# A list schedule planned with other durations, waits and priorities: clustered attention and an expert layer on one core

## The chip, the cores and the metric

The kernel runs on one core of a Trainium2 chip. A core has a tensor engine (PE in the profile), a vector engine (DVE), a scalar engine (ACT), GpSimd (POOL) and a queue that issues transfers (SP). Each engine works through its own queue in order; semaphores tie them together. The metric is the time of one execution on the device in microseconds, median of the runs shown.

## What is computed

Clustered attention over 4 batches, 8 heads, 768 tokens and 64 channels a head, followed by a layer with a rational activation. A query sees only the keys whose nearest centroid (of 16, by cosine) is its own.

```python
q_assign = np.argmax(np.einsum('bhsd,hcd->bhsc', q_n, c_n), axis=-1)
k_assign = np.argmax(np.einsum('bhsd,hcd->bhsc', k_n, c_n), axis=-1)
mask = q_assign[:, :, :, None] == k_assign[:, :, None, :]
scores = np.where(mask, scale * np.matmul(q, k.transpose(0, 1, 3, 2)), -1000000000.0)
attn = np.exp(scores - np.max(scores, axis=-1, keepdims=True))
attn = attn / (np.sum(attn, axis=-1, keepdims=True) + 1e-09)
x = np.matmul(attn, v)                    # then (3072 tokens, 512)
h = x @ w_in                              # (3072, 2048)
P = a[0] + a[1] * h + a[2] * h * h + a[3] * h * h * h
Q = 1.0 + np.abs(b[0]) * np.abs(h) + np.abs(b[1]) * h * h
out = (P / (Q + 1e-6)) @ w_out            # (3072, 512)
```

The weights arrive as float64 words.

## The kernel before

Every operand is split into two float16 parts (a high one and the rest), and each matrix product is made of three products of parts.

The work has four kinds. `weights` loads a chunk of w_in or w_out (8 chunks of 4 tiles), decodes the words on DVE, and splits them on ACT and POOL. `prep` prepares two heads of a batch: loads q, k and v, scales and splits them, finds the clusters, and turns the operands with DMA transposes. `v_scale` finds the scale of v in a batch from four loads of its own (tiles `rvm`); the loads for the work itself are `rv`, which has one buffer, so a pair's load waits until POOL has split the pair before it (`vlo`). `attend` handles two query tiles of each of two heads. `moe` handles 256 tokens in 8 groups of 256 hidden units.

For each of its 192 score tiles (4 batches x 4 head pairs x 6 query tiles x 2 heads) `attend` runs this chain. PE makes the scores (`s`, L861) into one of two score banks. DVE scales them and takes the row maximum (L877). ACT takes the exponential with the row sum (`su`). DVE makes the reciprocal in two small steps (L897, L902). The split follows: ACT writes the high part of the weights into `ah`, DVE writes the rest (L949). Then SP issues a DMA transpose of `ah` into `at` (L956), from which PE makes the product with v (`px`, L969). The tiles `ah` have two buffers, so ACT's part of a split waits until the transpose two tiles earlier has landed.

For each of its 96 groups `moe` makes `ph` on PE (L1028), two operations on ACT, a cubic on DVE (L1051, L1052), a square on POOL (L1057 to L1062), logarithm and exponential on ACT, a product on POOL (L1084), two more on DVE (L1099, L1106; every fifth of the former is on POOL), a split (`gh`, `gl`), and the product `po` on PE (L1127). All of a batch's four head pairs have to be done before its MoE begins, so the MoE of batch b runs beside the attention of batch b + 1, and the last one alone.

The order in each queue is set by a planner in the kernel (`Plan`). The body of the kernel only records operations: engine, an assumed duration in ns, tiles read and written, and a priority `vt`. `emit` then plays a list schedule over the engines with these durations: an operation is ready when its predecessors have ended and a time by engine (`LAT`) has passed; a transfer takes the issue time, a description time and its own duration; the rings of buffers and banks are counted. Of an engine's operations that can start within `look` ns the one with the least `vt` goes next:

```python
key = (max(start, now + self.look), o.vt, o.seq)
```

The order in which operations are picked is the order in which they are written to the program. The chip knows nothing of the assumed times: on it each engine runs its queue in that order and waits where it has to. `vt` counts MoE groups (8 a block of tokens, 24 a batch), shifted by an entry of the table `K` for the kind of operation, with further entries for the first batch (`.0`) and the last (`.3`).

Of the kernel before, what the change touches and what calls it, by code (L numbers as in the profile page):

```python
# [10 lines left out]
F32 = mybir.dt.float32  # L11
# [5 lines left out]
ALU = mybir.AluOpType  # L17
# [10 lines left out]
class Buf:  # L28
    """A tile that is allocated when the first operation on it is emitted."""
# [18 lines left out]
class Plan:  # L48
    """Records operations, then emits them in the order of a list schedule over the engines."""

    WINDOW = 3413.0
    LAT = {"PE": 200, "ACT": 155, "DVE": 130, "POOL": 80, "SP": 950}
# [5 lines left out]
    def op(self, eng, ns, fn, r=(), w=(), vt=0.0, claim=(), co=(), chain=None):  # L58
        """Reads r, writes w, reserves slots for claim. Of the tiles in co it writes a part of its own.
        Operations of a chain are emitted in their order."""  # L60
        o = Op()
        o.eng, o.ns, o.fn, o.vt, o.seq = eng, ns, fn, vt, len(self.ops)
        o.preds, o.succs, o.ready, o.after, o.then = set(), [], 0.0, None, []
        touched = {}
        for b in r:
            touched[b] = b.psum
        for b in w:
            touched[b] = True
        for b, wr in touched.items():
            if b not in co:  # L70
                o.preds.update(b.writers)
            if wr:
                o.preds.update(b.readers)
                if b in co and b.writers and not b.readers:
                    b.writers.append(o)
                else:
                    b.writers, b.readers = [o], []
            else:
                b.readers.append(o)
            b.left += 1  # L80
        for b in claim:
            if b not in touched:
                b.left += 1
                touched[b] = False
        o.preds.discard(o)
        if chain is not None:
            o.after = self.last.get(chain)
            self.last[chain] = o
        o.bufs = list(touched)
        self.ops.append(o)  # L90
        return o

    def emit(self):
# [15 lines left out]
        def slot_time(o):  # L109
            """When the ring slots that o still needs are free; None: not known yet."""  # L110
            t, need = 0.0, {}
            for b in o.bufs:
                if b.ring is None or b in held:
                    continue
                f = freed.setdefault(b.ring, [0.0] * b.cap)
                i = need.get(b.ring, 0)
                if len(f) <= i:
                    return None
                t = max(t, f[i])
                need[b.ring] = i + 1  # L120
            return t
# [3 lines left out]
        def clock(start, ns):  # L125
            """How long the tensor engine takes from start: half its clock after an idle window."""
            t = start
            while ns > 0:
                i = int(t // self.WINDOW)
                for n in range(max(warm) + 1, i + 1):  # L130
                    u = busy.get(n - 1, 0.0) / self.WINDOW
                    warm[n] = u > (0.46 if warm[n - 1] else 0.8)
                f = 1.0 if warm[i] else 2.0
                step = min(ns * f, (i + 1) * self.WINDOW - t + 1e-3)
                busy[i] = busy.get(i, 0.0) + step
                ns -= step / f
                t += step
            return t - start
# [50 lines left out]
def clustered_attention_moe_kernel(  # L189
# [53 lines left out]
    def half(b, i):  # L243
        """A part of b with its own dependencies; its operations claim b."""
# [978 lines left out]
```

## Time and profile before

| | us |
|---|---|
| median of 3 runs | 1087.58 (1087.26 to 1088.86) |
| span of the profiled execution | 1086.1 |
| DVE busy | 947.5 (87%) |
| PE busy | 846.7 (78%) |
| ACT busy | 790.9 (73%) |
| POOL busy | 729.9 (67%) |
| DMA queue, share of 16 engines | 67.9% |

The profiled execution took 1086.1 us from its first to its last instruction; what lies around it is the difference to the runs' own times, 1.5 us at the median. In the views below a tile's name stands without its buffer number, a line of the kernel as L949, and L303 is the helper through which all ACT operations are recorded, so that its groups are told apart by their tiles. A wait is written "engine, tile, line <- what released it". DMA share is the mean busy share of the core's 16 DMA engines.

### The profile page before, as it was taken

Reading aid. Unit: us, or ns where it says so; the run is one execution under the profiler, and the core shown is the slowest. Engines: PE = TensorE matmul, PEld = TensorE weight load, DVE = VectorE, ACT = ScalarE, POOL = GpSimd, SP = SyncE. Lnnn points to the kernel's source line nnn. Section 1 sums busy time; section 2 is a strip of 40 time slices with the busy share of each in tenths; the row PEclk is TensorE's granted clock in tenths of the full one; section 3 lists DMA queues with packets and bytes.
Section 4 is the critical chain, followed back from the end, with each engine's and each line's share of the span. In section 5 each row is a group of like instructions: output and inputs, shape, how many; then the busy total and the mean of one; then the engine's idle time right before and its main releaser. Section 6 shows DMA issues by size and latency. Waiting matters only on the chain. (4 is left out here: it accounts for less than half of the span.)

```text
span 1086.1 us, 19660 instructions
## 1 busy us (share of the span) xinstructions
PE 846.7 (78%) x6925; PEld 550.9 (51%) x6925; DVE 947.5 (87%) x1877; ACT 790.9 (73%) x1347; POOL 729.9 (67%) x741
## 2 busy tenths in 40 slices
PE   1244554556689898898988988988888889999997
PEld 1122332334455565555655565645655656576664
DVE  6488998878899898889999898989999999888886
ACT  3376765758878878678877878778888778776663
POOL 3656464637776878767897687848787888445553
PEclk9957676667899999999999999999999999999999
DMA  6499998899957777595786886686777675630000
GB/s 188 142 212 201 227 233 199 203 214 207 195 108 127 151 137 133 118 157 93 148 135 121 152 134 154 117 181 131 132 155 138 106 138 102 116 64 1 21 20 20
DMA packets 427922, 150.22 MB, mean 138 GB/s; under 512 B 404272, under 2 KB 420656, under 8 KB 427824
## 3 DMA queue, kind: packets, MB, share of 16 engines
q1 hardware_dynamic: 427824, 148.98, 67.9%
q8 instruction: 54, 0.88, 0.3%
q14 instruction: 44, 0.36, 0.1%
HBM read 41.98 MB, written 6.29 MB: 44 GB/s over the span
## 5 line engine op out<-in xcount | busy, mean ns | idle before, releaser
L861 PE MATMUL s<-sk,sq 128*128 128x384 f16 x768 | 176.4, 362 | 157.3 <-DVE ah L949 111.6
L1028 PE MATMUL ph<-x,win 128*128 128x256 f16 x2304 | 274.4, 276 | 7.1 <-DVE t L1052 3.0
L1028 PEld LDWEIGHTS <-win 128*128 128x128 f16 x2304 | 227.0, 99 | 53.1 <-issue 7.7
L1127 PE MATMUL po<-wout,gh 128*128 128x512 f16 x768 | 229.3, 380 | 1.0 <-ACT gh L1113 0.8
L303 ACT ACTIVATE s<-s,nm 128x768 f32<-128x768 f32 x192 | 167.5, 873 | 85.3 <-DVE s L877 72.2
L949 DVE SCALAR_TENSOR_TENSOR ah<-s,su,ah 128x768 f16<-128x768 f32 x192 | 190.8, 1010 | 40.1 <-ACT ah L303 39.2
L303 ACT ACTIVATE ah<-s,su 128x768 f16<-128x768 f32 x192 | 169.2, 899 | 47.2 <-DMA at<-ah 22.1
L877 DVE TENSOR_SCALAR_CACHE_REDUCE s<-s,cc 128x768 f32<-128x768 f32 x192 | 192.4, 1017 | 11.8 <-PE s L861 11.4
L861 PEld LDWEIGHTS <-sq 128*128 128x128 f16 x768 | 69.9, 104 | 239.7 <-DVE ah L949 137.0
L1127 PE MATMUL po<-wout,gl 128*128 128x512 f16 x384 | 146.2, 381 | 5.4 <-POOL gl L1116 3.5
L969 PE MATMUL px<-at,vhi 128*64 128x256 f16 x1152 | 115.7, 297 | 15.7 <-DMA at<-ah 9.8
L1057 POOL TENSOR_SCALAR s<-u,gk 128x512 f32<-128x512 f32 x84 | 80.5, 958 | 66.0 <-ACT u L303 65.7
L1060 POOL TENSOR_TENSOR s<-s,u 128x512 f32<-128x512 f32 x84 | 113.7, 1353 | 7.0
L1084 POOL TENSOR_TENSOR s<-s,u 128x512 f32<-128x512 f32 x72 | 96.8, 1348 | 30.2 <-ACT u L303 29.8
L1116 POOL TENSOR_TENSOR gl<-t,gh 128x512 f16<-128x512 f32 x72 | 86.2, 1201 | 43.9 <-ACT gh L1113 28.0
L1127 PEld LDWEIGHTS <-gh 128*128 128x128 f16 x768 | 73.5, 98 | 71.8 <-issue 2.9
L969 PEld LDWEIGHTS <-vhi 128*64 128x64 f16 x1152 | 73.2, 118 | 41.3 <-issue 14.0
L969 PE MATMUL px<-at,vlo 128*64 128x256 f16 x576 | 93.1, 294 | 0.0
L1106 DVE SCALAR_TENSOR_TENSOR t<-s,t 128x512 f32<-128x512 f32 x84 | 85.6, 1020 | 3.6 <-POOL s L1084 1.5
L1099 DVE SCALAR_TENSOR_TENSOR t<-t,gk,u 128x512 f32<-128x512 f32 x70 | 68.4, 980 | 2.1 <-ACT u L303 2.1
L1052 DVE SCALAR_TENSOR_TENSOR t<-t,gk,ph 128x512 f32<-128x512 f32 x84 | 62.8, 748 | 3.0
L303 ACT ACTIVATE t<-ph,gk 128x512 f32<-128x512 f32 x84 | 65.0, 778 | 0.0
(177 smaller groups left out, 1477.8 us busy)
## 6 DMA issues: line engine op xcount, KB each, us to landing
rwi<-in_moe_w_in_dram SPq DMA_DIRECT2D x16, 512.0 KB, 4.6
rwo<-in_moe_w_out_dram SPq DMA_DIRECT2D x16, 512.0 KB, 5.0
rv<-in_v_dram SPq DMA_DIRECT2D x16, 384.0 KB, 4.1
rq<-in_q_dram SPq DMA_DIRECT2D x32, 192.0 KB, 3.0
rk<-in_k_dram SPq DMA_DIRECT2D x32, 192.0 KB, 3.2
rvm<-in_v_dram SPq DMA_DIRECT2D x16, 384.0 KB, 4.1
out_dram<-ob SPq DMA_DIRECT2D x24, 256.0 KB, 2.3
at<-ah SPq DMA_TRANSPOSE x192, 4.1
```

The costliest lines, as they stand in the source:

```text
L303: lambda: nc.scalar.activation(out=out(), in_=in_(), func=func, **{a: (x() if callable(x) else x) for a, x in kw.items()}),
L861: nc.tensor.matmul(sc.ap[:, i, :SH], lhsT=st["q" + x].ap[:, j, t, :], rhs=st["k" + x].ap[:, j, ks, :].rearrange("p t c -> p (t c)"), start ...
L877: lambda nm=nm, view=view: ts(out=view(), in0=view(), scalar1=cc.ap, scalar2=None, op0=ALU.mult, op1=ALU.min, accum_out=nm.ap),
L949: lambda part=part, view=view, su=su: stt(out=part(1), in0=view(), scalar=su.ap, in1=part(0), op0=ALU.mult, op1=ALU.subtract),
L969: nc.tensor.matmul(px.ap[j * D : (j + 1) * D, :], lhsT=vv.ap[:, j, kt, :], rhs=at[j].ap[:, p_, kt].rearrange("p t c -> p (t c)"), start=(i ...
L1028: nc.tensor.matmul(ph.ap[:, fi * TW : (fi + 1) * TW], lhsT=win[:, wpart, c, f * P : (f + 1) * P], rhs=xs[c].ap[:, xpart], start=(i == 0), ...
L1057: nc.gpsimd.tensor_scalar(out=s.ap, in0=u.ap, scalar1=col("b1r")(), scalar2=col("b0r")(), op0=ALU.mult, op1=ALU.add)
L1060: nc.gpsimd.tensor_tensor(out=s.ap, in0=s.ap, in1=u.ap, op=ALU.mult)
L1084: lambda u=u, s=s: nc.gpsimd.tensor_tensor(out=s.ap, in0=s.ap, in1=u.ap, op=ALU.mult),
L1106: lambda t=t, s=s: stt(out=t.ap, in0=s.ap, scalar=2.0, in1=t.ap, op0=ALU.subtract, op1=ALU.mult),
L1116: lambda gl=gl, t=t, gh=gh, e=(nc.vector if tail else nc.gpsimd): e.tensor_tensor(out=gl.ap, in0=t.ap, in1=gh.ap, op=ALU.subtract),
L1127: nc.tensor.matmul(po[ti].ap, lhsT=gg.ap[:, cs], rhs=wout[:, wpart, f, :], start=(i == 0 and f % (cw if apart else NF) == 0), stop=(i == 2 ...
```

## The change

No operation is added, removed or changed, and every engine's queue has as many rows after as before (PE 13747, DVE 1677, ACT 1108, POOL 734, SP 384). What changes is what the planner assumes:

- `LAT`, the time from an operation's end to its successor on another engine, is raised for ACT, DVE and POOL.
- The assumed durations of nearly all operations are replaced. Those of ACT and DVE are set to what the profile shows for the group, less 93 ns on ACT and 65 ns for each some 700 ns on DVE, taken off in `op`. The transposes go from 1344 to 2200 ns, half of an attention product (`px`) from 1296 to 1000.
- The table `K` has new numbers for nearly every kind of operation, `look` among them. Counts of buffers (`xn`, `NR`, `stk`) and shares of work between engines (`ghd`, `mulp`, `vsc`, `sgp`, `scp`) keep their values.
- Comments and docstrings are dropped; two line breaks move the numbers by two (L949 is L951 in the new file).

```diff
-    LAT = {"PE": 200, "ACT": 155, "DVE": 130, "POOL": 80, "SP": 950}
+    LAT = {"PE": 200, "ACT": 200, "DVE": 170, "POOL": 100, "SP": 950}
...
         o = Op()
+
+        ns -= {"ACT": 93, "DVE": 65 * max(1, round(ns / 700))}.get(eng, 0)
         o.eng, o.ns, o.fn, o.vt, o.seq = eng, ns, fn, vt, len(self.ops)
...
-    K = {'ghd': 0.25, 'p3': -265.35, 'max': -78.8, 'exp': -49.35, 'po': 3.6,
...
+    K = {'ghd': 0.25, 'p3': -1644.51, 'max': -150.93, 'exp': 33.42, 'po': 1831.34,
...
                 dve(
-                    925,
+                    1156,
                     lambda nm=nm, view=view: ts(
...
                 act(
-                    880, view, view, AF.Exp, [nm], [sc, su], u + kb("exp", b),
+                    1071, view, view, AF.Exp, [nm], [sc, su], u + kb("exp", b),
...
-                        784, lambda part=part: part(0), view, AF.Identity, [sc, su], [ah], u + kb("split", b), chain="split",
+                        899, lambda part=part: part(0), view, AF.Identity, [sc, su], [ah], u + kb("split", b), chain="split",
...
-                        930,
+                        1010,
                         lambda part=part, view=view, su=su: stt(
...
                 op(
-                    "SP", 1344,
+                    "SP", 2200,
                     lambda ah=ah, j=j, ti=ti: nc.sync.dma_start_transpose(
...
-            op("PE", 9 * 144, lambda k0=k0: av(k0, k0 + 3), [vhi, vlo, *at], [px], u, [x])
+            op("PE", 1000, lambda k0=k0: av(k0, k0 + 3), [vhi, vlo, *at], [px], u, [x])
...
             dve(
-                602,
+                932 if tail else 1020,
                 lambda t=t, s=s: stt(out=t.ap, in0=s.ap, scalar=2.0, in1=t.ap, op0=ALU.subtract, op1=ALU.mult),
```

Two places show what moves. The first is DVE's queue in the attention of batch 2 (tiles of a batch's number stand with it: `ah2_1_1_1` is batch 2, pair 1, query tile 1, head 1), beside the MoE of batch 1 (`t1_1_3` is its second block, group 3). Before:

```order
L877 TENSOR_SCALAR s2_1_1_1_6929,nm2_1_1_1_6942<-s2_1_1_1_6929,cc2_1_5512 128x2x384
L877 TENSOR_SCALAR s2_1_2_0_6936,nm2_1_2_0_6957<-s2_1_2_0_6936,cc2_1_5512 128x2x384
L702 TENSOR_SCALAR qsc2_3_6974<-sumq2_3_6955 128x1
L1051 SCALAR_TENSOR_TENSOR t1_1_3_6944<-ph1_1_3_6886,gk1_2539,t1_1_3_6944 128x512
L1052 SCALAR_TENSOR_TENSOR t1_1_3_6944<-t1_1_3_6944,gk1_2539,ph1_1_3_6886 128x512
L897 TENSOR_SCALAR su2_1_1_1_6959<-su2_1_1_1_6959 128x1
L1106 SCALAR_TENSOR_TENSOR t1_1_2_6780<-s1_1_2_6726,t1_1_2_6780 128x512
L897 TENSOR_SCALAR su2_1_2_0_6986<-su2_1_2_0_6986 128x1
L902 RECIPROCAL su2_1_1_1_6959<-su2_1_1_1_6959 128x1
L902 RECIPROCAL su2_1_2_0_6986<-su2_1_2_0_6986 128x1
L949 SCALAR_TENSOR_TENSOR ah2_1_1_1_7008<-s2_1_1_1_6929,su2_1_1_1_6959,ah2_1_1_1_7008 128x768
L949 SCALAR_TENSOR_TENSOR ah2_1_2_0_7019<-s2_1_2_0_6936,su2_1_2_0_6986,ah2_1_2_0_7019 128x768
```

After, around the same tile:

```order
L1054 SCALAR_TENSOR_TENSOR t1_1_1_6821<-t1_1_1_6821,gk1_2548,ph1_1_1_6716 128x512
L899 TENSOR_SCALAR su2_1_1_0_6849<-su2_1_1_0_6849 128x1
L879 TENSOR_SCALAR s2_1_1_1_6826,nm2_1_1_1_6868<-s2_1_1_1_6826,cc2_1_5508 128x2x384
L904 RECIPROCAL su2_1_1_0_6849<-su2_1_1_0_6849 128x1
L1101 SCALAR_TENSOR_TENSOR t1_1_0_6638<-t1_1_0_6638,gk1_2548,u1_1_0_6606 128x512
L1108 SCALAR_TENSOR_TENSOR t1_1_0_6638<-s1_1_0_6613,t1_1_0_6638 128x512
L899 TENSOR_SCALAR su2_1_1_1_6872<-su2_1_1_1_6872 128x1
L951 SCALAR_TENSOR_TENSOR ah2_1_1_0_6886<-s2_1_1_0_6781,su2_1_1_0_6849,ah2_1_1_0_6886 128x768
L904 RECIPROCAL su2_1_1_1_6872<-su2_1_1_1_6872 128x1
L879 TENSOR_SCALAR s2_1_2_0_6905,nm2_1_2_0_6916<-s2_1_2_0_6905,cc2_1_5508 128x2x384
L951 SCALAR_TENSOR_TENSOR ah2_1_1_1_6913<-s2_1_1_1_6826,su2_1_1_1_6872,ah2_1_1_1_6913 128x768
L704 TENSOR_SCALAR qsc2_3_6949<-sumq2_3_6919 128x1
```

Before, the split of `ah2_1_1_1` stands behind the two reciprocals of its pair, with nothing but the other tile's reciprocal between its own and itself; two maxima, then two reciprocals, then two splits stand together. After, the tiles of a pair are staggered, and a row maximum stands between this tile's reciprocal and its split.

The second place is SP's queue in the start, around the first transpose of attention weights (`at0_0_0_0`; `rwo` are w_out's words, `rwi` those of w_in, `sq2` and `sk2` the turned operands with the clusters). Before:

```order
L755 DMA_TRANSPOSE sq20_0_338<-tq20_0_151 128x12x128
L755 DMA_TRANSPOSE sk20_0_341<-tk20_0_161 128x12x128
L317 DMA rvm0_0_343<-in_v_dram 128x2x384
L317 DMA rvm0_1_365<-in_v_dram 128x2x384
L317 DMA rvm0_2_390<-in_v_dram 128x2x384
L317 DMA rvm0_3_428<-in_v_dram 128x2x384
L956 DMA_TRANSPOSE at0_0_0_0_444<-ah0_0_0_0_421 128x12x128
L755 DMA_TRANSPOSE sk10_1_450<-tk10_1_430 128x12x128
L317 DMA rk0_2_457<-in_k_dram 128x384 x2
L755 DMA_TRANSPOSE sq10_1_466<-tq10_1_446 128x12x128
L317 DMA rq0_2_468<-in_q_dram 128x384
L317 DMA rwi2_0_479<-in_moe_w_in_dram 128x1024
```

After:

```order
L319 DMA rwo3_0_259<-in_moe_w_out_dram 128x1024
L319 DMA rwo3_1_263<-in_moe_w_out_dram 128x1024
L319 DMA rwo3_2_353<-in_moe_w_out_dram 128x1024
L757 DMA_TRANSPOSE sq20_0_359<-tq20_0_151 128x12x128
L757 DMA_TRANSPOSE sk20_0_362<-tk20_0_161 128x12x128
L319 DMA rwo3_3_366<-in_moe_w_out_dram 128x1024
L319 DMA rv0_1_374<-in_v_dram 128x2x384
L319 DMA rwo2_0_382<-in_moe_w_out_dram 128x1024
L319 DMA rv0_2_443<-in_v_dram 128x2x384
L958 DMA_TRANSPOSE at0_0_0_0_454<-ah0_0_0_0_437 128x12x128
L319 DMA rwo2_1_459<-in_moe_w_out_dram 128x1024
L757 DMA_TRANSPOSE sk10_1_480<-tk10_1_435 128x12x128
```

Before, the four loads for v's scale (`rvm0`) stand ahead of the first transpose of attention weights. After, they have moved ahead of all of w_out's words, and the loads of v for the second and third pair (`rv0_1`, `rv0_2`) stand ahead of that transpose.

## Rows read from the trace of the kernel before

**Rows 1.** the page, part 1: busy us, share of the span, instructions

```profile
PE 846.7 (78%) x6925; PEld 550.9 (51%) x6925; DVE 947.5 (87%) x1877; ACT 790.9 (73%) x1347; POOL 729.9 (67%) x741
```

**Rows 2.** busy us by stretch: PE, PEld, DVE, ACT, POOL, PEclk, DMA share, GB/s

```profile
0.00:50.00 50.00, 7.95 (x83) 5.43 (x84) 27.96 (x67) 15.55 (x27) 25.31 (x31) 1.00 0.57 164
50.00:300.00 250.00, 135.48 (x1116) 83.15 (x1114) 210.68 (x480) 175.83 (x323) 143.80 (x170) 0.69 0.94 209
300.00:950.00 650.00, 575.90 (x4831) 377.22 (x4830) 598.20 (x1174) 517.04 (x872) 495.13 (x494) 0.99 0.72 133
950.00:1087.00 137.00, 127.41 (x904) 85.09 (x900) 110.62 (x160) 82.49 (x127) 65.65 (x46) 1.00 0.10 25
```

**Rows 3.** chain that ended last, after 950 us: start us, us, what

```profile
966.99 2.59 PE po L1127 x12
969.58 2.62 PE ph L1028 x24
```

**Rows 4.** waits of DVE, whole span: us in total, times, longest us

```profile
DVE ah L949 <- ACT ah L303: 39.2, 50, 2.6
...
DVE s L877 <- PE s L861: 11.4, 19, 1.7
DVE su L897 <- ACT s L303: 9.5, 20, 1.3
```

**Rows 5.** waits of DVE from 300 to 950 us, the fourth and the last

```profile
DVE t L1099 <- ACT u L303: 2.1, 3, 1.1
...
DVE km L694 <- PE kt L692: 0.2, 1, 0.2
```

**Rows 6.** instructions of DVE at 600 us: start us, us, what [idle before]

```profile
599.61 0.68 DVE L1106 SCALAR_TENSOR_TENSOR t<-s,t 128x512 f32<-128x512 f32 x1
...
600.44 0.28 DVE L902 RECIPROCAL su<-su 128x1 f32<-128x1 f32 x2
603.28 1.02 DVE L949 SCALAR_TENSOR_TENSOR ah<-s,su,ah 128x768 f16<-128x768 f32 x1 [2.55 <-ACT ah L303]
```

**Rows 7.** instructions of ACT at 602 us, the same columns

```profile
602.35 0.90 ACT L303 ACTIVATE ah<-s,su 128x768 f16<-128x768 f32 x1 [1.50 <-DMA at<-ah]
```

**Rows 8.** waits of ACT, whole span

```profile
ACT ah L303 <- DMA at<-ah: 22.1, 30, 2.2
```

**Rows 9.** the page, part 6: DMA issues, us to landing

```profile
at<-ah SPq DMA_TRANSPOSE x192, 4.1
```

**Rows 10.** groups by line: busy us, mean ns | idle before

```profile
L949 DVE SCALAR_TENSOR_TENSOR ah<-s,su,ah 128x768 f16<-128x768 f32 x192 | 190.8, 1010 | 40.1 <-ACT ah L303 39.2
...
L303 ACT ACTIVATE ah<-s,su 128x768 f16<-128x768 f32 x192 | 169.2, 899 | 47.2 <-DMA at<-ah 22.1 <-DVE su L902 8.3 <-issue 6.2
...
L1106 DVE SCALAR_TENSOR_TENSOR t<-s,t 128x512 f32<-128x512 f32 x84 | 85.6, 1020 | 3.6 <-POOL s L1084 1.5 <-POOL t L1093 0.8
...
L1099 DVE SCALAR_TENSOR_TENSOR t<-t,gk,u 128x512 f32<-128x512 f32 x70 | 68.4, 980 | 2.1 <-ACT u L303 2.1
```

**Rows 11.** issues of SP in the start

```profile
46.69 8.53 SPq L317 DMA_DIRECT2D rvm<-in_v_dram  x4
56.70 1.27 SPq L956 DMA_TRANSPOSE at<-ah  x1
```

**Rows 12.** instructions of DVE at 417 us

```profile
417.32 1.67 DVE L1106 SCALAR_TENSOR_TENSOR t<-s,t 128x512 f32<-128x512 f32 x1
...
418.98 2.06 DVE L1106 SCALAR_TENSOR_TENSOR t<-s,t 128x512 f32<-128x512 f32 x1
```

**Rows 13.** instructions of POOL at 417 us

```profile
416.73 1.71 POOL L1084 TENSOR_TENSOR s<-s,u 128x512 f32<-128x512 f32 x1
418.41 2.08 POOL L837 TENSOR_TENSOR vlo<-rv,vhi 128x768 f16<-128x768 f32 x1
```

More of the change, by code (lines that the diff above doesn't have):

```diff
@@ L693, in prep @@
         m1 = buf([1, 1], F32, "m1", f"km{n}", 4)
-        dve(200, lambda: nc.vector.tensor_reduce(out=m1.ap, in_=pt.ap[0:1, :], axis=AX.X, op=ALU.max), [pt], [m1], u)
+        dve(270, lambda: nc.vector.tensor_reduce(out=m1.ap, in_=pt.ap[0:1, :], axis=AX.X, op=ALU.max), [pt], [m1], u)
         pb = misc([P, 1], F32, f"kb{n}")
-        op("PE", 65, lambda: nc.tensor.matmul(pb.ap, lhsT=ones[0:1, :], rhs=m1.ap, start=True, stop=True), [m1], [pb], u)
+        op("PE", 235, lambda: nc.tensor.matmul(pb.ap, lhsT=ones[0:1, :], rhs=m1.ap, start=True, stop=True), [m1], [pb], u)
         qs, ks = buf([P, 2], F32, "qsc", f"qsc{n}", 2), buf([P, 2], F32, "ksc", f"ksc{n}", 2)
@@ L749, in prep @@
                 )
-            dve(270, lambda nm=nm, hi=hi: nc.vector.tensor_copy(out=cols(nm + "2", 0), in_=cols(nm + "1", hi)), [one], [two], u)
+            dve(500, lambda nm=nm, hi=hi: nc.vector.tensor_copy(out=cols(nm + "2", 0), in_=cols(nm + "1", hi)), [one], [two], u)
         def turn(x, u):
             op(
-                "SP", 1344,
+                "SP", 2200,
                 lambda x=x: nc.sync.dma_start_transpose(
@@ L784, in prep @@
         u = vt + kb("p3", b, 3)
-        dve(465, lambda: nc.vector.tensor_reduce(out=mx.ap, in_=ptl.ap, axis=AX.X, op=ALU.max), [ptl], [mx], u)
-        dve(469, lambda: tt(out=df.ap, in0=ptl.ap, in1=spread(mx), op=ALU.is_ge), [ptl, mx], [df], u)
+        dve(548, lambda: nc.vector.tensor_reduce(out=mx.ap, in_=ptl.ap, axis=AX.X, op=ALU.max), [ptl], [mx], u)
+        dve(553, lambda: tt(out=df.ap, in0=ptl.ap, in1=spread(mx), op=ALU.is_ge), [ptl, mx], [df], u)
         op(
-            "POOL", 960,
+            "POOL", 1109,
             lambda: nc.gpsimd.tensor_tensor(
@@ L793, in prep @@
         )
-        dve(469, lambda: nc.vector.tensor_reduce(out=mx2.ap, in_=df.ap, axis=AX.X, op=ALU.max), [df], [mx2], u)
-        dve(469, lambda: tt(out=oh.ap, in0=df.ap, in1=spread(mx2), op=ALU.is_equal), [df, mx2], [oh], u)
+        dve(541, lambda: nc.vector.tensor_reduce(out=mx2.ap, in_=df.ap, axis=AX.X, op=ALU.max), [df], [mx2], u)
+        dve(917, lambda: tt(out=oh.ap, in0=df.ap, in1=spread(mx2), op=ALU.is_equal), [df, mx2], [oh], u)
         NCP = D // NCL
@@ L832, in prep @@
         else:
[L833 to L834 removed]
+            act(933, rvf, rvf, AF.Identity, [ev], [rv], vt + kb("p4", b, 4), scale=lambda: ev.ap[:, 1:2])
+            act(832, lambda: flat(vhi), rvf, AF.Copy, [rv], [vhi], vt + kb("p4", b, 4), chain="vhi")
         op(
[L836 removed]
+            "POOL", 1717,
             lambda: nc.gpsimd.tensor_tensor(out=flat(vlo), in0=rvf(), in1=flat(vhi), op=ALU.subtract),
@@ L901, in attend @@
                     )
-                dve(75, lambda su=su: nc.vector.reciprocal(out=su.ap, in_=su.ap), [], [su], u + kb("su", b))
+                dve(157, lambda su=su: nc.vector.reciprocal(out=su.ap, in_=su.ap), [], [su], u + kb("su", b))
                 ah = buf([P, 2, S], F16, "ah", f"ah{nn}", kn("ah", 2))
```

111 lines of the change are left out of this document (54 added, 57 removed).

## The prediction

> **What bounds the kernel now.** I read the busy shares first. VectorE (DVE) is busy 947.5 us, 87% of the span, ahead of TensorE with 78% [rows 1]. So I look for the time in which VectorE stands still: 1086.1 - 947.5 = 138.6 us. The table by stretches [rows 2] divides it. In the first 50 us 22.0 us are idle, while the first loads land. From 50 to 300 us (weights decoded beside the attention of batch 0) 39.3 us are idle, and the DMA share is 0.94: there the transfers are almost as full as VectorE (210.7 of 250). From 300 to 950 us (MoE of batches 0 to 2 beside the attention of batches 1 to 3) 51.8 us of 650 are idle, with a DMA share of 0.72 and TensorE at 575.9. After 950 us only the 24 groups of the last MoE are left, and there TensorE is the bound: 127.4 of the 136.1 us that remain, in a strict alternation of 2.62 us (ph) and 2.59 us (po) a group [rows 3]; 24 times 5.21 is 125.0 us.
>
> The change moves no work from one engine to another (every queue has as many rows after as before), so it can win only VectorE's idle time, and the waits say which. The longest by far is the split of the attention weights, L949, waiting for ScalarE's half of the same split: 39.2 us in 50 waits; the reciprocal's first step waits 9.5 us for the exponential, and the row maximum 11.4 us for the scores [rows 4]. In the 300 to 950 stretch ten further kinds of wait, from L1099's 2.1 us to km's 0.2, make 13.3 us together [rows 5].
>
> One such wait shows the mechanism. VectorE ends the two reciprocals (L902) at 600.72 us, and the next thing in its queue is the split of the same tile, which starts at 603.28 after 2.55 us of standing [rows 6]. ScalarE's half needs 0.90 us and began only at 602.35, 1.50 us late, because its output buffer was still being read by a DMA transpose [rows 7]. That second cause occurs 30 times, 22.1 us [rows 8]: there are two `ah` buffers, and a transpose takes a median of 4.1 us to land [rows 9]. So VectorE stands where the order puts the split too soon after its own reciprocal, or too soon after the split two tiles earlier.
>
> **The change part by part.** Names and dependencies stay; the numbers in the plan change and with them each queue's order. I count a queue's order with durations of this trace: the k-th row of VectorE's old order is its k-th instruction in the trace, so every wait has its place in the order.
>
> *Term 1, the split's wait.* For each tile I add the durations of VectorE's rows that stand between the reciprocal and the split (each by the mean of its group, as [rows 10], less the 0.07 us or so by which a row overlaps the next). Of 190 tiles of the old order (the first two left out), 23 have less than 0.7 us there, and these waited 22.0 us in sum, 0.96 each. 36 have 0.7 to 1.2 us and waited 7.2 us, 0.20 each. The other 131 waited 9.4 us, 0.07 each. So the count sorts the waits well: it should, since ScalarE's half lasts 0.899 us [rows 10] and both handoffs come on top. In the new order the same three classes hold 7, 27 and 156 tiles: 7 x 0.96 + 27 x 0.20 + 156 x 0.07 = 23 us, against 38.6: 15.3 us less. The buffers say the same: under 5.5 us from the split two tiles earlier are 30 tiles in the old order (18.1 us of the waits) and 11 in the new one. About a third, 5.4 us, lies in the start before the first MoE group, where the transfers are full; I take half of that, since a split that comes earlier there meets a transpose queued behind loads. Term 1 is 9.9 + 2.7 = 12.6 us. Its bounds: 0, if the next wait in line takes all of it, and 29, if the waits fall in the ratio in which the time missing below 1.2 us falls (29.5 us to 11.1 in sum) and the rest is hidden too.
>
> *Term 2, the neighbours in the same chain.* From row maximum to reciprocal the time missing below 1.2 us falls from 9.0 to 7.4 us in sum; by that ratio the 9.5 us become 7.8: 1.7 us. From a split to the maximum two tiles later (two score banks) the time missing below 1.5 us falls from 21.4 to 18.8; the 11.4 us become 10.0: 1.4 us. Bounds 0 and 21.
>
> *Term 3, the ten small kinds.* I have no count for them. They lie between 0 and 13.3 us [rows 5]; I take a quarter, 3.3 us, as the two ratios of term 2 (a fifth and an eighth) are the nearest thing to them and term 1's is larger.
>
> *The start.* SP's new order loads the four tiles for v's scale before the w_out tiles, and puts the loads of v for the second and third pair in front of the first transpose of attention weights. v has one buffer, so the third pair's load stands until GpSimd has split the second pair's v, and the transpose waits behind it. In the old trace SP spent 46.69 to 55.2 us on the four scale loads, ahead of that transpose at 56.70 [rows 11]; these now come sooner. The two effects have opposite signs and a like size, some 8 us by this row. I book 0, bounds -8 and +8.
>
> *The end.* The first groups of the last MoE stand at the same place behind the same last attention tiles, and TensorE's rows are the same. The new order runs ph of two groups, then po of two, where the old one alternates one and one. With the same work and a bound engine I book 0. What covers it are VectorE's 110.6 busy us against TensorE's 127.4 [rows 2]; if pairs cost half a microsecond each for want of a finished `gl`, that is 12 x 0.5 = 6 us more.
>
> Sum: 12.6 + 3.1 + 3.3 = 19.0 us. The profiled span of 1086.1 becomes 1067.1; the median of the runs, 1087.58, lies 1.5 us above that span, so **1068.6 us**.
>
> [...] The table of durations is made of means, and one of them is no property of its operation. L1106 takes 0.68 us in one call [rows 6], 1.67 and 2.06 us in two calls that start while GpSimd's L1084 and L837 are running [rows 12, 13], and 1.02 in the mean [rows 10]. [...]
>
> **The rivals.**
>
> *A, overlap with GpSimd takes the gain (slower).* L1106 and L1099 are 84 + 70 = 154 calls. If the new order sets them beside GpSimd more often, busy time grows where I count on idle time: 19.0 us over 154 calls, 0.12 us a call, decides. At 0.2 us a call the time is 1068.6 + 30.8 = 1099 us. For it: the plan gives each call one duration whatever runs beside it, and the spread from 0.68 to 2.06 us is there. Against it: the calls and GpSimd's load are the same, and GpSimd is busy 495 of 650 us in the middle [rows 2], so a call meets it about as often in any order. Chance 0.11.
>
> *B, the waits return (no change).* What VectorE no longer waits for at L949 it waits for at the next row, because something behind it, the DMA transposes or the scores, sets the pace. Time 1087 us. For it: ScalarE's late start above was itself a DMA's. Against it: between 300 and 950 us neither DMA (0.72) nor TensorE is full. Chance 0.08.
>
> *C, the whole chain is freed (faster than forecast).* The split's waits fall by 29 us, those of term 2 by 4, the small ones by 5, and the start counts in full: 38 us, 1050 us. For it: VectorE is 92% busy in the middle, so 52 us are there to be had. Against it: 37 us must come from waits of which the count moves less than half. Chance 0.16.
>
> **How the numbers follow.** The forecast (19.0 us won, give or take the 8 us of the start and the 6 of the end, so 5 to 27) has 0.65. Faster by over 0.2% (about what a measurement of this kernel can tell from no change, 2.2 us) are the forecast and C: 0.81. Within it is B: 0.08. Slower is A: 0.11. The predicted time is the forecast's, 1068.6. The range leaves out A and what might lie beyond C: it goes from 1049 us, just under C, to B's 1087.
>
> **What would show it.** Right: in the new profile L949 waits about 23 us for ScalarE instead of 39, the waits of ScalarE's half for the transposes fall from 22 to some 12 us, VectorE's idle time between 300 and 950 us falls from 52 to about 37, and its busy sum stays within 10 us of 947. A would show as L1106 and L1099 with means above 1.14 and 1.10 us and a busy sum over 965. B would show as the same idle sum under other names, with L877 waiting for scores. An end that TensorE needs more than 131 us for, or a first MoE group later than now, would make the terms that I booked at 0 wrong.

## The result and the profile after

The changed kernel takes 1076.86 us (median of 4 runs, 1075.24 to 1077.87) where the kernel before took 1087.42 us beside it (median of 4 runs): a ratio of 0.9901, with a 95% interval from 0.9884 to 0.9918. That is 10.6 us won; 19.0 were forecast, and the time lies in the range. The profiled execution took 1075.5 us, against 1086.1.

In the changed kernel every line number is 2 higher: L949 is L951, L877 is L879, L897 is L899, L1051 is L1053, L1099 is L1101, L1106 is L1108. The page's part 1 answers to [rows 1]:

```profile
PE 851.7 (79%) x6925; PEld 555.1 (52%) x6925; DVE 938.3 (87%) x1877; ACT 790.6 (74%) x1347; POOL 711.3 (66%) x741
```

and the four stretches to [rows 2]:

```profile
0.00:50.00 50.00, 9.60 (x83) 5.80 (x84) 27.72 (x70) 21.13 (x39) 23.96 (x31) 1.00 0.71 198
50.00:300.00 250.00, 144.12 (x1169) 91.18 (x1170) 216.66 (x493) 176.92 (x321) 152.88 (x178) 0.71 0.97 206
300.00:950.00 650.00, 582.04 (x4905) 383.49 (x4905) 599.55 (x1178) 521.97 (x883) 488.75 (x493) 0.98 0.72 134
950.00:1087.00 137.00, 115.98 (x774) 74.63 (x770) 94.39 (x138) 70.55 (x106) 45.71 (x41) 0.98 0.03 12
```

VectorE's idle time is 1075.5 - 938.3 = 137.2 us, and it was 138.6. The gain on the page is 9.2 us of busy time and 1.4 of idle time, though the change was to win idle time. Between 300 and 950 us VectorE is idle 50.5 us; it was 51.8, and some 37 were forecast. The waits of VectorE over the whole span show why (us in total, times, longest), beside [rows 4]:

```profile
DVE ah L951 <- ACT ah L305: 23.4, 35, 2.0
DVE s L879 <- PE s L863: 16.1, 21, 2.5
DVE t L1053 <- ACT t L305: 11.5, 14, 1.3
DVE sk L1053 <- ACT sk L305: 8.6, 9, 1.9
...
DVE su L899 <- ACT s L305: 6.7, 15, 1.1
```

The wait at the split went from 39.2 to 23.4 us, which is what term 1 counted. But VectorE waits 4.7 us more for scores, and the first polynomial step now waits 20.1 us for ScalarE (t and sk), where it waited 2.2 us before. ScalarE's wait for the transposes, which answers to [rows 8], fell little:

```profile
ACT ah L305 <- DMA at<-ah: 19.3, 17, 3.8
```

Of the groups by line, these two answer to L1106 and L1099 in [rows 10] (busy us, mean ns, idle before):

```profile
L1108 DVE SCALAR_TENSOR_TENSOR t<-s,t 128x512 f32<-128x512 f32 x84 | 75.1, 896 | 4.5 <-POOL t L1095 2.6
...
L1101 DVE SCALAR_TENSOR_TENSOR t<-t,gk,u 128x512 f32<-128x512 f32 x70 | 73.9, 1057 | 3.6 <-ACT u L305 3.4
```

Fixed windows hold different work in the two kernels, so I cut both spans at points of the work: the first polynomial step of the first MoE group and of the last batch. The windows of VectorE (length, busy us, instructions, then TensorE's granted clock, DMA share and GB/s) before:

```profile
0.00:271.60 271.60, 215.08 (x502) 0.74 0.87 203
271.60:945.80 674.20, 617.63 (x1210) 0.98 0.72 135
945.80:1086.10 140.30, 114.75 (x167) 1.00 0.13 30
```

and after:

```profile
0.00:263.90 263.90, 211.38 (x491) 0.73 0.91 204
263.90:932.80 668.90, 617.95 (x1225) 0.97 0.74 139
932.80:1075.50 142.70, 108.99 (x165) 0.99 0.11 26
```

The start is 7.7 us shorter, the middle 5.3 us shorter with the same busy time, and the end 2.4 us longer, although VectorE is busy 5.8 us less there. In idle time of VectorE that is 4.0 us less, 5.6 less and 8.2 more, so the sum over the span hides what the first two stretches won. A stretch of one profile is sure to some 3 us only: in the profile of a later run with the same order up to the last split, the start took 267.0 us and the middle 671.7. In the middle, between those two points, VectorE's longest waits were before:

```profile
DVE ah L949 <- ACT ah L303: 25.8, 30, 2.6
DVE s L877 <- PE s L861: 4.4, 6, 1.7
DVE su L897 <- ACT s L303: 4.3, 11, 1.0
```

and are after:

```profile
DVE ah L951 <- ACT ah L305: 13.4, 23, 2.0
DVE s L879 <- PE s L863: 8.9, 13, 2.5
DVE t L1053 <- ACT t L305: 3.9, 7, 1.3
DVE t L1101 <- ACT u L305: 3.4, 5, 1.3
DVE t L1108 <- POOL t L1095: 2.6, 2, 1.8
DVE tk L746 <- ACT tk L305: 2.6, 2, 2.4
DVE su L899 <- ACT s L305: 2.5, 7, 0.6
```

The split's wait fell by 12.4 us there and all waits together only from 48.5 to 43.3 us: other waits in the same queue grew by 7.2 us. The two orders differ everywhere, so these rows alone do not show that it is the same time that moved; the third buffer below, which leaves the order as it is, comes nearer to that.

In the end the chain that ended last shows the pairs (start us, us, what):

```profile
965.91 5.24 PE ph L1030 x48
971.15 5.18 PE po L1129 x24
...
991.99 2.60 PE po L1129 x12
...
996.01 0.58 ACT ob L305
...
996.63 2.10 PE po L1129 x6
```

A pair costs TensorE what two groups cost in [rows 3], 5.24 for 2 x 2.62 and 5.18 for 2 x 2.59. What is lost lies between: from 994.59 to 996.63 us TensorE does nothing, until ScalarE has copied a finished product out of its bank (`ob`).

### The profile page after: what moved, and what is told of

Read it like the earlier page. It is cut to its first block, busy times and chain, and to the rows that moved or that the text cites. A ratio compares the mean times of both kernels' runs of the same rounds, so it can differ in the third digit from the quotient of the medians.

```text
span 1075.5 us, 19599 instructions
## 1 busy us (share of the span) xinstructions
PE 851.7 (79%) x6925; PEld 555.1 (52%) x6925; DVE 938.3 (87%) x1877; ACT 790.6 (74%) x1347; POOL 711.3 (66%) x741
## 4 chain that ended last, share of the span: by engine, by line
DVE 30%; PE 30%; ACT 12%; issue 10%; DMA 8%; POOL 8%; SPq 1%; ACTq 0%; DVEq 0%; POOLq 0%
PE ph L1030 11%; PE po L1129 11%; DVE ah L951 7%; DVE s L879 6%; PE s L863 4%; DMA at<-ah 4%; ACT ah L305 3%; PE px L971 3%; DVE t L1053 2%; DVE t L1101 2%; ACT u L305 2%; ACT s L305 2%; DVE t L1054 2%; DVE t L1108 2%; DVE tq L746 1%
## 5 line engine op out<-in xcount | busy, mean ns | idle before, releaser
L863 PE MATMUL s<-sk,sq 128*128 128x384 f16 x768 | 180.2, 364 | 134.6 <-DVE ah L951 109.1
L951 DVE SCALAR_TENSOR_TENSOR ah<-s,su,ah 128x768 f16<-128x768 f32 x192 | 192.8, 1010 | 24.6 <-ACT ah L305 23.4
L879 DVE TENSOR_SCALAR_CACHE_REDUCE s<-s,cc 128x768 f32<-128x768 f32 x192 | 193.9, 1017 | 17.2 <-PE s L863 16.1
L305 ACT ACTIVATE ah<-s,su 128x768 f16<-128x768 f32 x192 | 171.1, 897 | 47.4 <-DMA at<-ah 19.3
L971 PE MATMUL px<-at,vhi 128*64 128x256 f16 x1152 | 120.4, 303 | 14.9 <-DMA at<-ah 13.8
L1118 POOL TENSOR_TENSOR gl<-t,gh 128x512 f16<-128x512 f32 x72 | 89.4, 1244 | 38.3 <-ACT gh L1115 27.9
L1059 POOL TENSOR_SCALAR s<-u,gk 128x512 f32<-128x512 f32 x84 | 73.1, 870 | 44.8 <-ACT u L305 44.6
L971 PEld LDWEIGHTS <-vhi 128*64 128x64 f16 x1152 | 76.6, 121 | 44.3 <-issue 26.8
L971 PE MATMUL px<-at,vlo 128*64 128x256 f16 x576 | 96.7, 299 | 0.0
L1108 DVE SCALAR_TENSOR_TENSOR t<-s,t 128x512 f32<-128x512 f32 x84 | 75.1, 896 | 4.5 <-POOL t L1095 2.6
L305 ACT ACTIVATE u<-ph,gk 128x512 f32<-128x512 f32 x84 | 57.5, 685 | 28.4 <-PE ph L1030 28.0
L1101 DVE SCALAR_TENSOR_TENSOR t<-t,gk,u 128x512 f32<-128x512 f32 x70 | 73.9, 1057 | 3.6 <-ACT u L305 3.4
L1053 DVE SCALAR_TENSOR_TENSOR t<-ph,gk,t 128x512 f32<-128x512 f32 x84 | 62.4, 743 | 11.8 <-ACT t L305 11.5
```

The costliest lines, as they stand in the source:

```text
L305: lambda: nc.scalar.activation(out=out(), in_=in_(), func=func, **{a: (x() if callable(x) else x) for a, x in kw.items()}),
L863: nc.tensor.matmul(sc.ap[:, i, :SH], lhsT=st["q" + x].ap[:, j, t, :], rhs=st["k" + x].ap[:, j, ks, :].rearrange("p t c -> p (t c)"), start ...
L879: lambda nm=nm, view=view: ts(out=view(), in0=view(), scalar1=cc.ap, scalar2=None, op0=ALU.mult, op1=ALU.min, accum_out=nm.ap),
L951: lambda part=part, view=view, su=su: stt(out=part(1), in0=view(), scalar=su.ap, in1=part(0), op0=ALU.mult, op1=ALU.subtract),
L971: nc.tensor.matmul(px.ap[j * D : (j + 1) * D, :], lhsT=vv.ap[:, j, kt, :], rhs=at[j].ap[:, p_, kt].rearrange("p t c -> p (t c)"), start=(i ...
L1101: lambda t=t, u=u, col=col: stt(out=t.ap, in0=t.ap, scalar=col("a0r")(), in1=u.ap, op0=ALU.add, op1=ALU.mult),
```

## Experiments

Since the operations are the same and are recorded in the same sequence, an order can be replayed and spliced. In the runs marked "replay" the list schedule is replaced by a table of the operations' sequence numbers:

```diff
-        while todo:
...
+        rank = {s: i for i, s in enumerate(ORDER)}
...
+        left = sorted(self.ops, key=lambda o: rank[o.seq])
...
+        while left:
+            o = next(o for o in left if not o.wait and fits(o))
```

Here `fits` asks for free ring slots. Line numbers in these kernels are 28 higher than in the changed kernel. Every ratio stands to the kernel before on the same chip; "at 1087.4" is that ratio times before's 1087.4 us. The times of runs that the expectations name are medians as measured, up to 1 us above these.

| run | ratio (95%) | at 1087.4 |
|---|---|---|
| changed kernel | 0.9901 (0.9884 to 0.9918) | 1076.6 |
| changed start, then old order | 1.0035 (1.0020 to 1.0051) | 1091.2 |
| the same, seam mended | 1.0063 (1.0043 to 1.0084) | 1094.3 |
| the same, work on values kept too | 1.0071 (1.0047 to 1.0094) | 1095.1 |
| old start, then changed order | 0.9979 (0.9958 to 0.9999) | 1085.1 |
| changed order, old last stretch | 0.9875 (0.9856 to 0.9895) | 1073.8 |
| the same, 8 scores earlier | 0.9893 (0.9864 to 0.9922) | 1075.8 |
| changed order, third ah buffer | 0.9885 (0.9868 to 0.9902) | 1074.9 |
| old order, third ah buffer | 0.9944 (0.9924 to 0.9963) | 1081.3 |
| changed order, old last stretch, third ah buffer | 0.9827 (0.9804 to 0.9850) | 1068.6 |
| durations alone | 1.0232 (1.0203 to 1.0262) | 1112.6 |
| priorities alone | 1.0184 (1.0156 to 1.0213) | 1107.4 |

### Which stretch holds the gain

Replays. Each kernel holds its table of numbers written out; the lines below say how the table was made. A is the changed kernel's order and B that of before; `i` and `j` stand at the first polynomial step in A and in B, `k` behind the last split.

```diff
-ORDER = A
+ORDER = A[:i] + [o for o in B if o not in A[:i]]
```

```diff
-ORDER = A
+ORDER = B[:j] + [o for o in A if o not in B[:j]]
```

```diff
-ORDER = A
+ORDER = A[:k] + [o for o in B if o not in A[:k]]
```

> The operations come in the changed kernel's order up to the first polynomial of the first MoE group, then in the order of before. By milestones of VectorE (first polynomial of batch 0, 1, 2, 3; last split; end) the changed kernel was 7.7 us ahead at the first polynomial, 12.9 us ahead by the last batch, and 10.6 us ahead at the end. Theory (the stretches add up, a head start lasts): 1087.4 - 7.7, so 1078 to 1082 us, with the first polynomial near 264 us against 271.6 us. Rival (the head start is lost, since the middle waits for other things once it starts earlier): 1085 to 1088 us, with the first polynomial near 264 us all the same and a longer middle.

> The order of before up to the first polynomial of the first MoE group, then the order of the changed kernel. Theory (stretches add up): 1076.9 + 7.7, so 1083 to 1086 us; VectorE's wait for ScalarE's half at the split near 26 us over the span (23.4 in the changed kernel, 39.2 before). Rival (what the start gains is not the start's): 1076 to 1079 us.

> The changed kernel's order up to the last split of the last attention, then the order of before for what is left, so that the products of the last MoE groups alternate again (one first product, one second product) where the changed kernel sets them in pairs. From the last split to the end it took 127.2 us before and 130.5 us in the changed kernel. Theory (the pairs cost the difference): 1073 to 1075 us, with a last stretch of 127 to 128.5 us and the waits for sk near zero (8.6 us in the changed kernel, 0.2 before). Rival (the last stretch is longer because work was left over to it by the order ahead of it, not by the pairs): 1076 to 1078 us, with a last stretch of 130 us or more.

The second came out as the theory had it: 1085.1 us. With the old start the rest of the changed order wins 2.3 us, just clear of the error, so the changed start is worth some 8.5 us, give or take 3, in the company of the rest. The third too: 1073.8 us, and from the last split to the end 125.8 us instead of 130.5, shorter than the 127 to 128.5 expected. TensorE's waits in that stretch say what the pairs do (us in total, times, longest). In the changed kernel:

```profile
PE po L1129 <- ACT ob L305: 4.1, 2, 2.1
```

and with the old last stretch, where the wait for `ob` is gone:

```profile
PE po L1157 <- DVE gl L1146: 1.5, 1, 1.5
```

The two waits of the changed kernel stand where one block of 256 tokens ends and the next begins (the first is the gap above):

```profile
996.63 0.59 PE L1129 MATMUL po<-wout,gh 128*128 128x512 f16 x2 [2.05 <-ACT ob L305]
...
1042.20 0.59 PE L1129 MATMUL po<-wout,gh 128*128 128x512 f16 x2 [2.05 <-ACT ob L305]
```

With pairs, the new block's `po` comes right behind the old block's and has to wait until ScalarE has emptied the banks. With alternation a `ph` of 2.62 us stands between, and in the kernel before the wait for `ob` is 0.2 us there. These 4.1 us are most of the 4.7. VectorE waits some 21 us in that stretch with pairs and 13 with alternation, but TensorE, busy 121.0 of the 130.5 us with pairs and 119.4 of 125.8 with the old last stretch, sets the time there.

The first run was slower than before (1091.2 us), where the theory had 1078 to 1082 us and the rival 1085 to 1088; its first polynomial step came at 275.3 us and not near 264. VectorE stood 7.3 us in one wait at the maximum behind the values' squares (vm), right behind the seam, since the order of before asks for it early and the changed order loads its data late. I moved what lay across the seam:

```diff
+late = [o for o in B[:j] if o not in A[:i]]
-ORDER = A[:i] + [o for o in B if o not in A[:i]]
+ORDER = A[:i] + [B without A[:i], each of late ahead of the operation that follows it in A]
```

> As the run with the changed kernel's start and the order of before behind it, but the 20 operations that the order of before has ahead of the first polynomial and the changed order behind it (the loads, absolute values and maximum of the values of batch 1 among them) keep the changed kernel's places. In the earlier run VectorE stood 7.3 us at the maximum of those values (vm), whose load had only just been issued, right at the seam. Theory (stretches add up; the seam cost the head start): first polynomial at 263 to 267 us, no wait of over 3 us for vm there, 1077 to 1083 us. Rival (the middle of before cannot use the head start): first polynomial at 263 to 267 us, 1085 to 1089 us.

Now the first polynomial step came at 262.9 us, but VectorE stood 17.0 us at vm, 11.8 of it in one wait, and the time was 1094.3 us, beyond both texts. In the next run the 16 operations on the values' scale of batches 2 and 3 were added to `late`:

> The changed kernel's start and the order of before behind it, a third time: now all the work on the scale of the values of batches 2 and 3 (loads, squares, maximum and what follows, 16 operations each) keeps the changed kernel's places as well, later than in the order of before. In the two earlier runs VectorE stood 12.2 and 17.0 us at the maximum of those values behind the seam. Theory (only these loads, put off by the changed start, ate the head start): waits for vm under 6 us, 1077 to 1083 us. Rival (the head start is other work put off, which the order of before then has in its way wherever it is set): waits for vm under 6 us, but other idle time in their place, 1085 to 1092 us.

The waits for vm were gone, and the time was no better: 1095.1 us, beyond the rival's 1092 as well. Some 30 us behind the first polynomial step VectorE stood for something else (an instruction of VectorE: start us, us, what, and the idle time before it):

```profile
297.99 0.75 DVE L1129 SCALAR_TENSOR_TENSOR t<-t,gk,u 128x512 f32<-128x512 f32 x1 [6.48 <-ACT u L333]
```

As the rival had it, other idle time took the place of the waits for vm: between the two cuts VectorE is idle 72.0 us in this run and 72.1 in the one before it, against 56.6 in the kernel before. Work put off is only a small part of the head start: four of VectorE's operations, nine instructions of some 2.7 us in all, stand behind the first polynomial step in the changed order. The stretches do not add up in this direction. What exactly the old middle lacks is left open after three splices.

### Either part of the change alone

The durations alone, against the changed kernel:

```diff
-    K = {'ghd': 0.25, 'p3': -1644.51, 'max': -150.93, 'exp': 33.42,
+    K = {'ghd': 0.25, 'p3': -265.35, 'max': -78.8, 'exp': -49.35,
...
```

The priorities alone, against the kernel before:

```diff
-    K = {'ghd': 0.25, 'p3': -265.35, 'max': -78.8, 'exp': -49.35, 'po': 3.6,
...
+    K = {'ghd': 0.25, 'p3': -1644.51, 'max': -150.93, 'exp': 33.42, 'po': 1831.34,
...
```

> One part of the change alone: the planner has the new durations and latencies, the priorities are those of before. In this order 61 of the 192 tiles have under 1.2 us of VectorE's work between the reciprocal and the split (58 before, 30 in the changed kernel, counted with the planner's new durations), and the products of the last groups alternate as before. Theory (the two parts fit only each other): VectorE's wait at the split stays at 32 to 42 us, the last stretch stays near 127 us, and the time is 1082 to 1092 us. Rival (the truer durations carry the gain whatever the priorities): 1074 to 1080 us, with the wait at the split near 25 us.

> The other part alone: the new priorities, with the durations and latencies of before. 55 of the 192 tiles have under 1.2 us of VectorE's work between the reciprocal and the split (58 before, 30 in the changed kernel), and the products of the last groups come in pairs as in the changed kernel. Theory (the two parts fit only each other): wait at the split 30 to 40 us, a last stretch near 130 us, 1087 to 1097 us. Rival (the priorities carry the gain): 1074 to 1080 us.

Both are far slower than either kernel, by more than the theory allowed. The waits of VectorE name different causes. With the durations alone (planner's numbers new, `K` old):

```profile
DVE s L879 <- PE s L863: 34.7, 43, 2.4
DVE ah L951 <- ACT ah L305: 26.7, 43, 1.7
```

With the priorities alone (lines as before):

```profile
DVE ah L949 <- ACT ah L303: 40.7, 50, 2.9
DVE t L1051 <- ACT t L303: 17.9, 12, 2.0
```

The new durations alone lowered the wait at the split to 26.7 us, as the rival had it, but the wait for scores is three times that of before, and no time was won. The priorities alone left the split as it was and brought VectorE's waits at the first polynomial step. Cut as above, the two lose in different places. With the durations alone the start is 5.4 us shorter than before and the middle 32.7 us longer. With the priorities alone the start is 20.3 us longer (37 more of VectorE's instructions stand in it), the middle 6.8 us shorter and the end 5.0 us longer; from the last split to the end it takes 146 us, where 130 were expected. As a whole, neither part won anything without the other.

### The two buffers

```diff
-                ah = buf([P, 2, S], F16, "ah", f"ah{nn}", kn("ah", 2))
+                ah = buf([P, 2, S], F16, "ah", f"ah{nn}", kn("ah", 3))
```

> The changed kernel's order, operation by operation, with a third buffer for the halves of the split (ah 3 in place of 2), so that ScalarE needs not wait until the transfer of two tiles before has left its buffer. ScalarE's waits for that transfer were 22.1 us before and 19.3 us in the changed kernel, 17 of them. Theory (the waits lie on the path of the split, and a third of them or more reaches VectorE): those waits go to under 3 us, VectorE's wait at the split falls from 23.4 to 10 to 18 us, and the time is 1066 to 1073 us. Rival 1 (the transfer itself is late: its reader, the attention's second product, waits instead): ScalarE's waits go, the time is within 2 us of 1076.9 us. Rival 2 (other waits of VectorE take their place, those for scores first): the wait at the split falls as in the theory, waits for scores rise by as much, 1075 to 1078 us.

> The order of before, operation by operation, with a third buffer for the halves of the split (ah 3 in place of 2). ScalarE waited 22.1 us, 30 times, until a transfer had left its buffer, and VectorE waited 18.1 us at the splits of 30 tiles that stand under 5.5 us behind the split of two tiles before. Theory 1 (those 18.1 us are the two buffers' doing): VectorE's wait at the split falls from 39.2 to 20 to 26 us, the time to 1072 to 1079 us. Theory 2 (as the third buffer showed in the changed order, where it took away 19.3 us of ScalarE's waits, 4.0 us of VectorE's and 0.9 us of the time): wait at the split 33 to 38 us, 1083 to 1087 us.

> The changed kernel's order with the alternating last stretch of before, and a third buffer for the halves of the split. The alternating stretch alone gave 1074.5 us, the third buffer alone 1075.9 us, the changed kernel 1076.9 us. Theory (both add up): 1072 to 1074 us. Rival (the third buffer gives nothing): 1074 to 1076 us.

In both orders ScalarE's waits for the transfer vanish (1.0 us is left in the changed order, 0.6 in the old one). In the old order VectorE's wait at the split follows:

```profile
DVE ah L979 <- ACT ah L333: 24.6, 36, 1.7
...
DVE s L907 <- PE s L891: 12.4, 21, 1.5
```

It falls from 39.2 to 24.6 us, by 14.6, near the 18.1 us that the prediction's count gave to the buffers; the time falls by 6.1 us (4.0 to 8.3 by the interval), between the two theories. So a third buffer does to the old order's split what the new plan does. Not all of the wait became time: in this profile VectorE's idle time fell by 7.5 us (from 138.6 to 131.1), so about half of the 14.6 us came back in other rows. In the middle of the changed kernel 12.4 us at the split went with 5.2 us in all, a similar share.

In the changed order the wait falls from 23.4 to 19.4 us only, less than the theory and the second rival had it; waits for scores rise from 16.1 to 18.2, and the time is within the error of the changed kernel, which is nearest to the second rival. With the old last stretch and the third buffer together the time is 1068.6 us, below the interval of the changed kernel and below what either text expected: a version that beats both. There the third buffer is worth 5.2 us (1073.8 to 1068.6), give or take some 3; in the changed kernel it was 1.7 us with a like error, so whether it is worth more there is not shown.

### The waits for scores

A replay of the changed order with the old last stretch, in which 8 scores stand ahead of the one or two operations of TensorE that stood ahead of them:

```diff
+for s, ahead in eight:
+    for o in ahead: ORDER.remove(o)
+    ORDER[ORDER.index(s) + 1 : ORDER.index(s) + 1] = ahead
```

(This too says how the table was made.)

> The order with the alternating last stretch (1074.5 us), but for the 8 tiles behind 300 us whose scores VectorE waited for while TensorE was still in an operation of another kind after the bank had come free: on TensorE their scores come ahead of the one operation (where the bank was free for over 1.4 us: the two operations) that stood ahead of them. These 8 waits took 6.6 us in the changed kernel's profile and 9.2 us in that of the order with the alternating tail. Theory (the waits for scores are made by TensorE's order and are on the path): waits for scores fall by 5 to 9 us, the time is 1066 to 1071 us. Rival (TensorE's work that is put off is then waited for by ScalarE and VectorE, since TensorE is busy 582 of 650 us there): waits for scores fall all the same, others rise, 1072 to 1077 us.

The waits for scores fell from 20.4 us (changed order, old last stretch) to 15.3, those of the polynomial rose from 2.3 to 6.3, and the time stayed within the error. The lines, with the scores earlier:

```profile
DVE s L907 <- PE s L891: 15.3, 21, 1.7
...
DVE t L1081 <- ACT t L333: 6.3, 7, 1.7
```

The rival held. With TensorE busy 582 of 650 us in the changed kernel, what it does earlier for one wait it seems to do later for another.

### The price of overlap with GpSimd

A program of its own, which computes nothing of the reference:

```diff
+    dve(d, 24)
+    for _ in range(12):
+        ptt(out=e, in0=d, in1=c, op=ALU.mult)
...
+    dve(h, 24, z, ps)
```

> Not the kernel's computation: a program of repeated instructions on 128 x 512 float32 tiles, which writes one tile of numbers to every part of the output. VectorE's operation of line 1106 (two operands from SBUF) 24 times alone; GpSimd's product 12 times and its tensor-scalar operation 12 times alone; then 36 of VectorE beside 24 of GpSimd, all from SBUF; then 24 of VectorE with one operand from PSUM beside 12 products of GpSimd. Theory (VectorE's 9.2 us less busy time in the changed kernel is less overlap with GpSimd): alone 0.65 to 0.75 us, beside GpSimd 1.0 us or more on the mean with some at 1.6 to 2.1 us, and GpSimd's products longer too. Rival (the operands' places or the order on VectorE itself make them long): the same 0.65 to 0.75 us beside GpSimd.

Groups of VectorE's instructions in order of time (start us, us for the whole group, what). Alone:

```profile
2.98 17.39 DVE L49 SCALAR_TENSOR_TENSOR d<-a,b 128x512 f32<-128x512 f32 x24
```

beside GpSimd's products:

```profile
48.83 22.36 DVE L49 SCALAR_TENSOR_TENSOR d<-a,b 128x512 f32<-128x512 f32 x14
```

beside GpSimd's tensor-scalar operations:

```profile
71.23 12.14 DVE L49 SCALAR_TENSOR_TENSOR d<-a,b 128x512 f32<-128x512 f32 x12
```

and with one operand in PSUM, beside GpSimd's products:

```profile
84.20 17.30 DVE L49 SCALAR_TENSOR_TENSOR h<-z,ps 128x512 f32<-128x512 f32 x24
```

GpSimd's product in the same stretches: alone, beside VectorE's two operands of SBUF, beside the PSUM operand:

```profile
20.45 16.00 POOL L53 TENSOR_TENSOR e<-d,c 128x512 f32<-128x512 f32 x12 [20.00 <-DVE d L49]
...
50.60 20.05 POOL L59 TENSOR_TENSOR e<-h,c 128x512 f32<-128x512 f32 x12
...
84.25 16.08 POOL L65 TENSOR_TENSOR w<-z,c 128x512 f32<-128x512 f32 x12 [1.42 <-DVE z L63]
```

A call takes 0.72 us alone, about 1.6 to 1.67 beside products (the 14 include one that ran nearly alone), 1.01 beside tensor-scalar operations, and 0.72 again with a PSUM operand. The other 10 of the 36 calls ran earlier than planned, beside the tensor-scalar operations that were to run alone, and took 0.98 us each. The prices are those of the theory. In the changed kernel the calls of L1108 pay them less often:

```profile
L1108 DVE SCALAR_TENSOR_TENSOR t<-s,t x84: 666/692/1943, 280.0 to 1057.3; 128x512 f32<-128x512 f32 x84
```

The columns are the least, median and largest time of a call in ns. The median of 692 is near the call alone, which in this program is busy for 0.69 us (16.6 us for the 24 calls; 0.72 is from one start to the next); before, it was 981. Counted in the two traces, 18 of the line's 96 calls (on `t` and `sk`) ran beside no instruction of GpSimd before and 43 do after; these took 0.68 us in the mean in both traces, the others 1.08 before and 1.03 after.

## Why the prediction was right, and where not

*Term 1 was right as a wait and too large as a gain.* 23 us at the split were forecast, and 23.4 came; in the middle 12.4 us less where 9.9 were booked. It holds class by class: counted in the changed kernel's trace, 6, 26 and 158 tiles fall into the three classes and waited 7.1, 4.8 and 11.5 us, where 6.7, 5.4 and 10.9 were forecast. The step that failed is the one from wait to time, which was taken as one to one. In the middle all waits together fell by 5.2 us, and with the third buffer in the old order idle time fell by 7.5 us for 14.6 at the split. The idle time between 300 and 950 us, which was to fall to about 37 us, is 50.5. The upper bound of 29 does not follow from the ratio given for it, which takes 24 of the 38.6 us. The grounds for term 1 held but for one: ScalarE's waits for the transposes went to 19.3 us and not to 12. There are 17 now instead of 30, and the longest is 3.8 us instead of 2.2, which a count of tiles under 5.5 us does not show.

*Term 2.* The exponential's part came (9.5 to 6.7 us, forecast 7.8). The scores' part had the wrong sign: 16.1 us, forecast 10.0. The count looked at the room between a split and the maximum two tiles later on VectorE and not at what TensorE has queued ahead of the scores; moving 8 scores ahead of that took 5.1 us from these waits and brought others.

*Term 3 had the wrong sign.* All waits of the middle but those at the split, for scores and for the exponential made 48.5 - 25.8 - 4.4 - 4.3 = 14.0 us and make 43.3 - 13.4 - 8.9 - 2.5 = 18.5 us. A share of the waits was booked as won with no count behind it.

*The start, booked at 0 with bounds of 8, won 7.7 us in this profile, near the bound, and not by what was named.* The first transpose of attention weights is issued at 56.38 us, where it was 56.70 [rows 11], so the two effects on SP's queue leave it where it was. VectorE's wait for the first weights of w_out is 4.2 us instead of 13.3, but that for the values' maximum is 4.7 instead of 0.6, and small ones are new: in the first 50 us VectorE is idle 22.3 us, and it was 22.0. The gain lies behind 50 us. From there to the first polynomial step VectorE has 3.5 us less to do (some 2.7 of it the work put off) and 4.2 us less idle time, 3.3 of it at the split. The split's wait up to the first polynomial step was and is:

```profile
DVE ah L949 <- ACT ah L303: 11.7, 18, 2.0
...
DVE ah L951 <- ACT ah L305: 8.4, 11, 1.5
```

So much of what the start itself won is term 1 again, which had booked 2.7 us here. The splice gives the changed start 8.5 us, more than these 4.2; what makes the rest is open.

*The end, booked at 0 with up to 6 us of loss, lost 2.4 us.* The loss was priced as pairs that want for a finished `gl`; that wait is 0.3 us there. What came in its place are the two waits of 2.05 us for ScalarE's copy `ob`, where the blocks of tokens meet.

The sum closes for this profile: 19.0 forecast, 5.0 more from the start (7.7 against the 2.7 booked), 11.0 less from the middle (5.3 against 16.3), 2.4 less from the end, makes 10.6. That the time lies in the range is in part luck: a start that was booked at 0 made up for nearly half of what the middle failed to give.

*The rivals.* B held in part, with its sign: the same idle sum (137.2 us) under other names, the scores among them. It did not decide the time, because the start came in and the end lost little. A did not: L1108's mean is 0.90 us and L1101's 1.06, below the bounds of 1.14 and 1.10, and the busy sum moved by 9.2 us the other way, within the 10 that were allowed. 5.8 us of that are in the end, where an instruction of GpSimd ran beside 20 of the 24 calls of the line before and beside 4 of 24 after, and there TensorE sets the time, so it won nothing: with the old last stretch the busy sum is back at 946.4 us and the kernel is faster. C needed waits to vanish and not to move.

## What to carry to other kernels

Where two engines are nearly full (here VectorE 92% and TensorE 90% in the middle), a wait that is taken away at one row can come back in part at others: with the third buffer about half of it did, so a count of waits should not be booked one to one. A plan's durations and its priorities were one thing here: either alone cost some 2%. After a change of order, cut the span at points of the work and look at each stretch by itself, and there at the engine that sets the time: the loss of 2.4 us in the last one, two waits of TensorE, could be undone with a short edit and gave, with a third buffer, the best version.

## What the hardware showed

In the program above, what a call of VectorE and a product of GpSimd cost each other depended on where VectorE's operands were. With both operands in SBUF, 14 calls took 22.36 us and, beside them, 13 products 21.65 us, from 49.00 to 70.65. A pair took 20.05 / 12 = 1.67 us. The two one after the other would be 0.72 + 16.00 / 12 = 2.06 us (an estimate from their times alone), so each slowed the other, but the pair was 0.4 us shorter than that. With one operand in PSUM neither was slowed: 17.30 us for 24 calls and 16.08 us for 12 products at once, where each alone took 17.39 and 16.00.
